# An adaLN block with dilated window attention and a token-mixing MLP: filling matmuls moved ahead of the first transposes, loads reordered, and a new issue order

## The chip, the cores and the metric

The kernel runs on one core of one Trainium2 chip. The metric is device microseconds of one execution, taken as the median of several runs. "Span" is the time from the first to the last instruction of one profiled execution; the time of a run is a little longer than its span.

The engines are named as the profile names them: PE multiplies matrices (PEld is its weight load), DVE, ACT and POOL work on elements, SP issues most of the DMA transfers. Each engine runs its own instructions in order and waits for the others through semaphores.

## The reference, cut to what matters

The input x has 2048 tokens of 512 features (bf16). A vector c gives six rows of modulation (scale, shift and gate for two branches).

```python
mod = (silu(c) @ w_mod).reshape(1, 6, 1, 512)
sa, ca, ga, sb, cb, gb = six rows of mod
h = layernorm(x) * (1 + ca) + sa
q, k, v = split(h @ wqkv)                  # 32 heads of 16
for each token: logits over 8 keys, at distances 0, 2, ..., 14 back
attn = softmax(logits * 16 ** -0.5)        # keys before the start are masked
x = x + ga * ((attn over v) @ wo)
h = layernorm(x) * (1 + cb) + sb
g = layernorm(h)
u = gelu(einsum('sd,sf->df', g, w1) + b1)  # mixes the 2048 tokens to 1792
y = einsum('df,fs->ds', u, w2) + b2        # and back to 2048 tokens
out = x + gb * y.T
```

## The kernel before, in words

Tokens are cut into 16 tiles of 128 and these into five chunks of 2, 4, 4, 4 and 2 tiles (`SIZES`, line 253). `build_chunk` (line 607) writes the work of one chunk:

- First layer norm: statistics (`ln1s`, on DVE, or with `:a` on ACT), reciprocal root on ACT (`rstd1_`, `rste1_`), then the normalised tile (`n1_`, on ACT, DVE or POOL).
- Transposition. Chunks 0 and 1 do it on PE (`tr0_0`, `tr1_0`, `tr1_2`), and the copy out of PSUM multiplies by `a1col`, the modulation scale plus one (`hT0_`, `hT1_`). Chunks 2 to 4 do it by transposing DMAs (`xt`), and use QKV weights that were multiplied by `a1col` instead (`wsc`).
- Projection on PE (`qkv{chunk}_{0 q, 1 k, 2 v}{part}`), copied out by ACT (`ev`). The q and v copies add a bias from the modulation shift (`qvb`, from `sab`).
- Scores: DVE multiplies q by eight shifted views of k (`qk`, four per chunk), and PE sums over a head (`red`). Softmax: max on DVE (`max`), subtracted on PE (`sub`), exponential on ACT (`exp`), sum on PE (`esum`), reciprocal on ACT (`rcp`, `rcq`), multiplied on DVE (`smB`).
- The softmax weights go through four DMAs to another layout (`a2_`), v through four others (`vd`). DVE multiplies them (`pv`, four per chunk), PE sums (`pvacc`), ACT copies (`oev`).
- Output projection with the residual (`wo`, `x1_`), second norm (`ln2`, `n2_`), modulation by rows (`aff`, `afb` on DVE), third norm (`ln3s`, `h3_`).

The MLP's first layer (`mlp1_{part}_{column block}_{first tile}`) needs tiles of `h3` as its reduction dimension, so its matmuls fill PE while the chunks run. Partial sums are parked in SBUF (`park`) and added later (`padd`); then `gelu`, then the second layer (`mlp2_`), the last arithmetic on DVE (`fin`) and the stores (`st_out`).

What sets the order is the string `ORDER` (line 180). Every step above is added to a graph by name, and `schedule` (line 87) checks that each name stands behind the names it depends on, picks PSUM and buffer slots in that order, and emits each step on its engine. A suffix picks an alternative: `:a`, `:d`, `:p` the engine, `:s` skip the step, `:q` write each product of 128 weight columns as four matmuls of 32 columns at four positions (`mm`, line 517). So each engine's queue, SP's DMA queue among them, is the list of names that fall to it, in the order of the string.

At the start, `ld_c` and the first x tiles are loaded, `cps` (one small matmul that turns c) leads to silu on ACT and DVE, and `modcols1`, `modcols0` (lines 553 and 556) multiply silu(c) with the modulation weights `ld_wmod1`, `ld_wmod0` for `a1col` and `sab`. The `warm` steps (line 523) are filling matmuls: they multiply the identity by itself, and nobody reads the product. `WARM` (line 267) gives how many matmuls each has. `warm0` is built apart (line 538): it stands behind `cps`, and by the key `wmA1` in front of `modcols1` and `modcols0`.

Of the kernel before, what the change touches and what calls it, by code (L numbers as in the profile page):

```python
# [180 lines left out]
halo0 ident ld_c act_table cps silu_exp ld_x1 ld_x0 ln1s0 ln1v0 ln1s1:a ln1v1 rstd1_0 rste1_0 ld_x_2_8 ld_x_1_2 nb1_0  # L181
consts ln1s9 silu_dve n1_1 n1_0:p tr0_0 ln1s8 ld_x_1_4 ln1s4:a ld_x_2_6 ln1s3:a warm0 ln1s5 ln1s7 ld_wmod1 ln1v5
ld_wmod0 modcols1 modcols0 ln1v9 ln1v8 ln1v4 ln1s2 ln1v2 ld_wqkv0 ln1v7 ln1v3 ln1s6 ln1v6 rstd1_1 rste1_1 nb1_1 n1_4:d
rstd1_2 rste1_2 n1_2:d n1_5:d nb1_2 ld_wqkv1 n1_3 n1_7 n1_6:d a1col hT0_2:d n1_9 tr1_2 tr1_0 hT1_1 wsc0_1:p hT0_1:d
sab hT0_0:d ld_x_3_12 hT0_3:d hT1_3:d qvb0 qvb_cp0 qkv0_00 warm6:s wsc1_3:a hT1_2:d qkv0_02 ev0_00 ld_wqkv2 qkv0_10
qkv0_12 ld_b2 ev0_10 ld_x_4_14 wsc1_2:p qkv0_20 wsc0_0 qvb1 ld_x_3_10 wsc0_3:p hT1_0:d ev0_02 wsc2_2:a ln1s13 ln1s12
ev0_12 ln1v12 ln1v13 wsc1_1:a qkv0_22 qk0_1 qkv1_13 ld_wmod2 ld_wo3 qk0_0 qk0_2 n1_8 red0_0 red0_1 ln1s11:a qkv1_03:q
qvb_cp1 qk0_3 xt6 red0_2 ld_wmod3 ev1_13 ev1_03 red0_3 mask wsc2_3:a ln1v11 ln1s10 ld_b1 ld_wo0 xt8 ev0_20 xt7 qkv1_11
ev1_11 ln1v10 max0 qkv1_01 ev1_01 rstd1_3 ev0_22 qk1_3 xt9 sub0 exp0 qkv1_00 ev1_00 qkv1_10 ev1_10 wsc1_0:a vd0_0
qk1_1 qkv1_02 esum0 rcp0 wsc0_2:p qk1_0 ev1_02 qkv1_12 qkv1_23 ld_wmod4 ld_wmod5 rcq0 ev1_12 qkv1_21 rste1_3 smB0  # L190
nb1_3 a2_0_0 ln1s15:a a2_0_2 qkv2_00 qk1_2 qkv2_10 n1_13:p red1_0 ev2_00 red1_1 ev2_10 red1_2 red1_3 ln1v15 a2_0_1
ev1_23 qkv2_13:q qk2_0 ev1_21 max1 modrow qkv1_20:q sub1:q ln1s14:a a2_0_3 pv0_0 wsc2_1:a halo_v1:a qkv1_22:q mrows
# [24 lines left out]
park0_8 ln2q13 pv4_3 park0_9 pvacc4_3 ld_w2_3 pv4_1 ld_w1_0_1664 oev4_2 pvacc4_0 ln2w12 warm4:s aff10 afb10 ld_w1_1_0
mlp1_0_12_6:q pvacc4_1 rstd2_12 rste2_12 nb2_12 n2_12:p ln3s10 mlp1_0_11_2:q oev4_0 ln3v10 wo15:q n2_13:p ld_row3
wo14:q mlp1_0_13_0:q mlp1_0_13_2:q ld_w2_0 x1_15:d ln3s11:a ln2m15 ln2q15 x1_14:d ln3v11 ln2w15 ln2m14 mlp1_0_11_6
mlp1_1_4_6 mlp1_0_13_6 aff12 ln2q14 rstd2_15 ln2w14 mlp1_1_1_6 afb12 rstd2_14 rste2_15 nb2_15 n2_15:p rste2_14  # L220
ld_w1_1_640 nb2_14 park0_10 warm5:s ln3s13 n2_14 ln3s12 rstd3_10 park0_11 aff14 rste3_10 ln3v13 park0_12 ln3v12
mlp1_1_2_6 afb14 aff15 rstd3_12 rste3_12 ln3s14 nb3_10 ln3v14 park0_13 mlp1_1_3_6 h3_10 rstd3_14 mlp1_1_0_6 afb15
ln3s15 ln3v15 mlp1_1_1_10 rstd3_15 rste3_15 mlp1_1_4_10 nb3_12:s rste3_14 mlp1_1_3_10 h3_13:d mlp1_1_0_10 mlp1_1_2_10
nb3_14:s h3_12:d mlp1_1_6_6 mlp1_1_6_10 nb3_15 h3_14:d padd1_0 mlp1_1_5_6 mlp1_1_5_10 h3_15 padd1_1 padd1_2 padd1_3
ld_w1_1_896 h3_11:p mlp1_1_7_10 padd1_7 gelu7 padd1_4 padd1_5 mlp1_1_8_10 mlp1_1_10_10 padd1_10 ld_w1_1_1408 padd1_6
ld_w1_2_0 big_done padd1_8 gelu10 mlp1_1_9_10 mlp1_1_11_10 mlp1_2_0_11 mlp1_2_2_11 mlp1_2_2_14 padd2_2 gelu8 padd1_9
# [12 lines left out]
def kernel(  # L239
# [24 lines left out]
    GRP=(2, 4, 4, 2, 1),  # L264
    XDMA=(2, 3, 4),
    INJ=(),
    WARM=(12, 2, 2, 2, 2, 2, 2, 2),
):
    nc = _OrderedNC(tc, 1)
    G = _Graph(dict(ps=6, big=NBIG, vd=NVD))  # L270
# [76 lines left out]
    add = G.add  # L347
# [681 lines left out]
```

## Time and profile before

| | |
|---|---|
| time, median of 3 runs | 198.08 us (197.78 to 198.33) |
| span of the profiled execution | 196.8 us |
| PE busy | 185.2 us (94%) |
| DVE busy | 156.6 us (80%) |
| ACT busy | 124.9 us (63%) |
| POOL busy | 19.9 us (10%) |
| chain of waits, by engine | PE 73%, DVE 13%, ACT 5%, issue 3%, DMA 2% |
| granted TensorE clock | 0.999 |

The profiled execution's own time is known only as its span; it is 1.3 us below the median of the runs. The busy time of PE counts the overlapped, modelled ends of matmuls, so 94% does not mean that PE works at its peak. In the page, a row of 40 digits cuts the span in slices of 4.92 us, and a digit is the busy share in tenths. In the timeline, the first column is the start and the second the length, from the start of the span; instructions that follow each other in one form are merged, "x12" is how many, and in brackets stands how long the engine was idle before and what released it. In the chain of waits, a row is start, length and what held the end at that time. Since almost every instruction is issued by one helper line (131), the tile names tell what an instruction is: `psS<-ident` a filling matmul, `big<-q_sb,k_f` a q·k product, `big<-a2sb,vD` a product with V, `lsb<-lsb,rb` the softmax multiply, `psS<-woq,o_sb` the output projection, `psS<-h,wst` and `psS<-gT,...` the MLP's two layers.

### The profile page before, as it was taken

To read this page: it belongs to the slowest core of one execution; us is meant where nothing else is said; L and a number is where in the kernel's file an instruction comes from. 1 tells how busy PE (TensorE), PEld (TensorE's weight loads), DVE (VectorE), ACT (ScalarE), POOL (GpSimd) and SP (SyncE) were. 2 spreads that over 40 slices of the span, in tenths; PEclk is the share of its full clock that TensorE was granted. 3 is DMA by queue.
4 is the path that set the end of the run, shared out by engine and by line. 5 is a ranking of instruction groups with operands and counts; after the bars stand their busy time and mean duration, and the time that the engine had idled before them with its cause. 6 is when DMAs were issued, how large, how long until landed. Compare 5 with 4: busy or idle time off the path is not lost.

```text
span 196.8 us, 4628 instructions
## 1 busy us (share of the span) xinstructions
PE 185.2 (94%) x1850; PEld 95.5 (48%) x1867; DVE 156.6 (80%) x244; ACT 124.9 (63%) x293; POOL 19.9 (10%) x38
## 2 busy tenths in 40 slices
PE   0699999999999999899999999999999999999994
PEld 0369554654444467244544454444444444444453
DVE  2888999999999999999999999965841633453664
ACT  6877999998999999999797889812760000000000
POOL 5123006320000005030000031200000000000000
PEclk9999999999999999999999999999999999999999
DMA  5998478778899732969674768888939293001112
GB/s 169 312 366 248 115 165 256 235 216 238 165 193 317 252 131 80 312 167 249 199 200 136 159 176 180 197 250 170 336 65 309 82 257 102 30 27 53 53 53 82
DMA packets 55369, 35.95 MB, mean 183 GB/s; under 512 B 24628, under 2 KB 52788, under 8 KB 55348
## 3 DMA queue, kind: packets, MB, share of 16 engines
q1 hardware_dynamic: 53468, 34.05, 63.2%
q10 hardware_dynamic: 1880, 1.61, 2.5%
q8 instruction: 14, 0.23, 0.5%
q14 instruction: 7, 0.06, 0.1%
HBM read 22.03 MB, written 2.10 MB: 123 GB/s over the span
## 4 chain that ended last, share of the span: by engine, by line
PE 73%; DVE 13%; ACT 5%; issue 3%; DMA 2%; SPq 1%; POOL 0%; DVEq 0%; ACTq 0%
PE psS L131 71%; DVE big L131 9%; DVE h L131 2%; PE psL L131 2%; ACT junk L131 1%; SPq L131 1%; DMA vD<-v_sb 1%; ACT xx L131 1%; DMA xx<-in_A_x_dram 1%; DVE m L131 1%; ACT o_sb L131 1%; ACT lsb L131 0%; DVE mv L131 0%; POOL h L131 0%; ACT v_sb L131 0%
## 5 line engine op out<-in xcount | busy, mean ns | idle before, releaser
L131 PEld LDWEIGHTS <-wst 128*128 128x128 bf16 (+1 forms) x566 | 35.5, 100 | 31.9 <-issue 1.3
L131 PE MATMUL psS<-h,wst 128*32 128x512 bf16 (+1 forms) x400 | 50.5, 379 | 0.4 <-issue 0.3
L131 DVE TENSOR_TENSOR big<-q_sb,k_f 128x4096 bf16<-128x4096 bf16 (+1 forms) x20 | 36.4, 1857 | 0.5 <-ACT k_f L131 0.5
L131 DVE TENSOR_TENSOR big<-a2sb,vD 128x4096 bf16<-128x4096 bf16 (+1 forms) x20 | 36.6, 1858 | 0.0
L131 DVE SCALAR_TENSOR_TENSOR h<-psS,bcol,rows_bc 128x512 f32<-128x512 f32 (+2 forms) x18 | 12.4, 690 | 24.2 <-PE psS L131 24.0
L131 PE MATMUL psS<-hT,w_qkv 128*32 128x512 bf16 (+3 forms) x414 | 28.7, 337 | 0.8 <-ACT v_sb L131 0.4
L131 PEld LDWEIGHTS <-w_qkv 128*32 128x32 bf16 (+1 forms) x462 | 19.9, 108 | 16.4 <-issue 2.7
L131 PE MATMUL psS<-gT,big 128*128 128x512 bf16 x109 | 24.3, 379 | 0.2
L131 POOL TENSOR_SCALAR h<-xx,rs,nb 128x512 bf16<-128x512 bf16 x6 | 10.6, 1777 | 84.2 <-DVE nb L131 84.2
L131 PEld LDWEIGHTS <-big 128*128 128x128 bf16 x144 | 12.0, 98 | 13.7 <-issue 0.5
L131 ACT ACTIVATE junk<-xx 128x512 bf16<-128x512 bf16 x28 | 17.7, 631 | 1.3 <-DVE xx L131 0.3
L131 ACT ACTIVATE h<-xx,nb,rs 128x512 bf16<-128x512 bf16 x22 | 17.2, 818 | 0.4 <-DVE nb L131 0.4
L131 PE MATMUL psS<-woq,o_sb 128*32 128x512 bf16 (+1 forms) x123 | 15.8, 380 | 0.4 <-ACT o_sb L131 0.4
L131 ACT ACTIVATE gT<-psS,bcol 128x512 bf16<-128x512 f32 x14 | 8.8, 686 | 10.6 <-DVE psS L131 10.6
L131 DVE TENSOR_TENSOR psS<-psS,gT 128x512 f32<-128x512 f32 x14 | 9.2, 695 | 6.3 <-PE psS L131 6.3
L131 DVE TENSOR_TENSOR h<-h,xx 128x512 bf16<-128x512 f32 (+2 forms) x18 | 11.4, 633 | 0.7
L131 ACT ACTIVATE q_sb<-psS,qvb 128x512 bf16<-128x512 f32 (+1 forms) x20 | 11.6, 603 | 0.3 <-PE psS L131 0.2
L131 PEld LDWEIGHTS <-group 128*32 128x32 bf16 x288 | 7.0, 96 | 9.8 <-issue 4.0
L131 PE MATMUL psS<-hT,wst 128*128 128x256 bf16 (+2 forms) x74 | 11.3, 333 | 0.1
L131 ACT ACTIVATE v_sb<-psS,qvb 128x512 bf16<-128x512 f32 (+1 forms) x20 | 11.2, 607 | 0.0
L131 DVE TENSOR_TENSOR h<-h,rows_bc 128x1024 bf16<-128x1024 bf16 (+2 forms) x14 | 10.5, 759 | 0.0
L131 ACT ACTIVATE k_f<-psS 128x512 bf16<-128x512 f32 x16 | 9.7, 606 | 1.1 <-PE psS L131 1.1
(90 smaller groups left out, 223.3 us busy)
## 6 DMA issues: line engine op xcount, KB each, us to landing
vD<-v_sb SPq DMA_DIRECT2D x12, 524.5 KB, 4.8
big<-in_B_w_dram SPq DMA_DIRECT2D x4, 896.0 KB, 7.5
vD<-v_sb SPq DMA_DIRECT2D x8, 268.5 KB, 3.1
wst<-in_B_w_dram SPq DMA_DIRECT2D x3, 640.0 KB, 5.4
xx<-in_A_x_dram SPq DMA_DIRECT2D x7, 256.0 KB, 5.6
wst<-in_B_w_dram SPq DMA_DIRECT2D x2, 800.0 KB, 4.7
gT<-in_w_mod_dram SPq DMA_DIRECT2D x3, 512.0 KB, 5.4
wst<-in_B_w_dram SPq DMA_DIRECT2D x2, 768.0 KB, 5.6
```

What stands on the lines that cost most here:

```text
L131: r = fn(*a, **k)
```

## The change

`WARM` goes from `(12, 2, ...)` to `(9, 1, 2, ...)`, `warm0` becomes a step like the others, without the key that held it in front of the modulation columns, and `ORDER` is replaced as a whole.

```diff
-    WARM=(12, 2, 2, 2, 2, 2, 2, 2),
+    WARM=(9, 1, 2, 2, 2, 2, 2, 2),
...
-        if w_ == 0:
-            f_warm0, s_w0 = f_warm, s_w
-            continue
...
-    add("pe", 0.216 * WARM[0], f_warm0, after=[G.ops[-1]], alloc=s_w0, frees=s_w0, writes=["wmA1"], name="warm0")
...
-    add("pe", 0.42, lambda: f_cols(1), reads=["sc", ("wmodA", 1), "wmA1"], writes=["wmA1"], alloc=s_m[1], name="modcols1")
+    add("pe", 0.42, lambda: f_cols(1), reads=["sc", ("wmodA", 1)], alloc=s_m[1], name="modcols1")
...
-    add("pe", 0.42, lambda: f_cols(0), reads=["sc", ("wmodA", 0), "wmA1"], frees=s_wm, alloc=s_m[0], name="modcols0")
+    add("pe", 0.42, lambda: f_cols(0), reads=["sc", ("wmodA", 0)], frees=s_wm, alloc=s_m[0], name="modcols0")
```

The start of the two strings, cut to the first lines (all of the rest differs too):

```diff
-halo0 ident ld_c act_table cps silu_exp ld_x1 ld_x0 ln1s0 ln1v0 ln1s1:a ln1v1 rstd1_0 rste1_0 ld_x_2_8 ld_x_1_2 nb1_0
-consts ln1s9 silu_dve n1_1 n1_0:p tr0_0 ln1s8 ld_x_1_4 ln1s4:a ld_x_2_6 ln1s3:a warm0 ln1s5 ln1s7 ld_wmod1 ln1v5
-ld_wmod0 modcols1 modcols0 ln1v9 ln1v8 ln1v4 ln1s2 ln1v2 ld_wqkv0 ln1v7 ln1v3 ln1s6 ln1v6 rstd1_1 rste1_1 nb1_1 n1_4:d
...
+ident ld_c cps act_table silu_exp ld_x0 ld_x1 ln1s0:a silu_dve ln1s1 ln1v1 ln1v0 ld_x_1_4 rstd1_0 rste1_0 ln1s4 nb1_0
+ln1s5 ld_x_1_2 ln1s2 ln1s3 ln1v2 ld_wmod1 ln1v5 consts n1_1 ln1v3 ln1v4 rstd1_1 rste1_1 ld_x_2_8 n1_0:p ld_x_2_6
+ld_wqkv1 warm0 tr0_0 nb1_1 n1_2 ln1s8:a ld_wmod0 ld_wqkv0 warm1 modcols1 a1col ld_x_3_10 ld_x_3_12 n1_5:d n1_3:d hT0_0
+n1_4:p ld_b1 wsc1_0:p warm2 tr1_2 ld_wqkv2 hT0_3:d ln1s6 hT0_2:d hT0_1:d ln1s7 ln1v8 wsc1_2:p tr1_0 ln1v7 ld_x_4_14
+qkv0_10 hT1_2 ln1s9 hT1_0 ln1v6 ln1v9 qkv0_12 modcols0 hT1_3 rstd1_2 rste1_2 ld_b2 hT1_1:d nb1_2 ev0_10 n1_9:d qkv1_10
...
```

What the new order does, in the words of the steps:

- Loads on SP: x0, x1, x tiles 4 and 5, 2 and 3, `wmod1`, x tiles 8 and 9, 6 and 7, `wqkv1` (K), `wmod0`, `wqkv0` (Q). Before: x1, x0, 8 and 9, 2 and 3, 4 and 5, 6 and 7, `wmod1`, `wmod0`, `wqkv0`, `wqkv1`.
- PE: `cps`, `warm0` (9 matmuls), `tr0_0`, `warm1` (1), `modcols1`, `warm2` (2), `tr1_2`, `tr1_0`, then the K projection of chunk 0 ahead of `modcols0` and of Q. Before: `cps`, `tr0_0`, `warm0` (12), `modcols1`, `modcols0`, `tr1_2`, `tr1_0`, `qvb0`, Q, K. The skipped `warm` steps stand at the end of the string, and the two matmuls of `warm1` behind the last product are gone.
- More steps are written with `:q`: 1829 matmuls of 32 columns and 561 of 128, for 1129 and 738. Neighbours on PE whose width differs go from 26 to 4.
- Engines: the norms `n1_4`, `n1_7`, `n1_8`, `n1_11`, `n2_0`, `n2_2`, `h3_13` and `h3_15` move to POOL, `n1_13` and `n2_5` leave it; `halo0` moves behind `n1_8` on POOL. Some statistics, norms, column scalings (`hT`) and weight scalings trade between DVE and ACT; `ev0_12` moves to DVE.
- `qk1_0` stands ahead of `max0` on DVE, `woq_s` ahead of the first `pv`. `mlp2` tiles, `st_out` stores and the late W1 and W2 loads stand in another order; the last tile's three pieces keep theirs.

101 lines of the change are left out of this document (50 added, 51 removed).

## The prediction

> **What bounds the kernel now.** I read the page first (the busy shares and the 40 slices), then the windows by stage, the chain of waits, and at last the timeline at each place where the chain changes engine.
>
> ```profile
> span 196.8 us, 4628 instructions
> DVE  2888999999999999999999999965841633453664
> ```
> ```profile
> 2.00:8.00 6.00, 1.71 (x11) 1.23 (x12) 3.65 (x10) 4.92 (x13) 2.06 (x14) 1.00 0.92 277
> 8.00:13.00 5.00, 5.00 (x38) 2.14 (x37) 4.29 (x19) 4.12 (x13) 0.00 (x0) 1.00 1.08 371
> 18.00:42.00 24.00, 23.63 (x305) 13.82 (x310) 23.89 (x23) 23.45 (x53) 5.90 (x2) 1.00 0.65 174
> 42.00:82.80 40.80, 39.12 (x605) 20.57 (x604) 40.73 (x34) 39.24 (x93) 2.90 (x2) 1.00 0.80 217
> 82.80:193.80 111.00, 110.33 (x833) 52.70 (x842) 78.88 (x145) 49.18 (x121) 5.11 (x6) 1.00 0.59 157
> ```
> ```profile
> 6.47 10.88 PE psS L131 x108
> ...
> 18.07 1.79 DVE big L131 x2
> ...
> 36.91 1.22 DVE big L131
> ...
> 82.77 7.30 PE psS L131 x33
> ```
> ```profile
> 184.51 9.30 PE L131 MATMUL psS<-gT,wst 128*128 128x512 bf16 x70
> ```
>
> A window's row gives PE, PEld, DVE, ACT and POOL busy, then clock, DMA share and GB/s. There are three regimes. Until 18 the loads feed everything (DMA share 0.92 and 1.08). From 18 to 82.8 DVE never rests (23.89 of 24.00, 40.73 of 40.80). From 82.8 to the last matmul (184.51 + 9.30 = 193.8) PE is busy 110.33 of 111.00, and 3.0 us of output work follow. DVE's slices (4.92 us each) stay full until about 125 us, so the two are in balance: PE's gain counts only as far as DVE's chain comes earlier too.
>
> **The change part by part.** Every sum is made against the profiled span of 196.8; the median of the runs, 198.08, stands 1.3 above it, and I carry the difference over unchanged.
>
> *The filling matmuls.*
>
> ```profile
> 2.20 0.18 PE L131 MATMUL psS<-ident,c_t 4*128 4x4 bf16 x1 [2.20 <-DMA c_t<-in_c_dram]
> ...
> 5.64 0.77 POOL L131 TENSOR_SCALAR h<-xx,rs,nb 128x512 bf16<-128x512 bf16 x1 [2.11 <-DVE nb L131]
> ...
> 6.47 1.03 PE L131 MATMUL psS<-ident,h 128*128 128x128 bf16 x8 [4.09 <-POOL h L131]
> ...
> 7.30 5.20 PE L131 MATMUL psS<-ident 128*128 128x512 bf16 x12
> ...
> 12.33 0.94 PE L131 MATMUL psS<-sc,big 128*128 128x1 bf16 x32
> ...
> 13.13 1.05 PE L131 MATMUL psS<-ident,h 128*128 128x128 bf16 x16
> ...
> 14.02 0.67 PE L131 MATMUL psS<-sab,wst 128*128 128x1 bf16 x16
> ...
> 14.55 3.66 PE L131 MATMUL psS<-hT,wst 128*128 128x256 bf16 x32
> ...
> 18.07 3.50 DVE L131 TENSOR_TENSOR big<-q_sb,k_f 128x2048 bf16<-128x2048 bf16 x3 [0.51 <-ACT k_f L131]
> ```
>
> Before, twelve fillers of 0.43 us (5.20/12) stand between the first transposes and the modulation columns. After, nine stand behind the silu product: 2.4 + 9 x 0.43 = 6.3, inside PE's wait of 4.09 for the first normalised tile at 6.42. They cost nothing; were that tile 0.2 us earlier, they would begin to. Three more fillers stand in gaps where PE waits for loads. So 5.2 us leave PE's path, and what is late next is the loads.
>
> *The loads.*
>
> ```profile
> wst<-in_A_wqkv_dram SPq DMA_DIRECT2D x2, 512.0 KB, 8.3
> ```
>
> They land in issue order at 277 GB/s to 8 and 371 after. Before, the first QKV weight is complete at 2.88 MB: by these rates 11.3, by its landing (issued at 4.8, 8.3 median less 0.5) 12.6, so completion lags 1.3. After, the modulation weights for the scale complete at 1.31 MB (8.0), the K weights at 2.36 MB (11.2), the Q weights at 3.41 MB (14.0). K of chunk 0 so starts at 11.2, 3.3 ahead of the first projection now (14.55); but Q must wait for its bias product at 14.5, and runs 15.0 to 16.0. Its copy on ACT (behind one K copy, one norm and one weight scaling) ends at 17.3. DVE's own queue ahead of the first q·k product, counted in the instruction orders, holds 11 statistics instead of 9 and one K copy more, three norms and four column scalings instead of four and seven: 0.2 us more in all. Starting 0.6 earlier and waiting as long, it is there at 17.7. **First q·k: 17.7 for 18.07, -0.4**, though PE then has nearly three projections of chunk 1 behind it (0.87 each at 217 ns for 512 columns, below) that it has not begun now: some 2 us ahead.
>
> *First softmax and first products with V.*
>
> ```profile
> L131 DVE TENSOR_TENSOR big<-q_sb,k_f 128x4096 bf16<-128x4096 bf16 x12 | 27.1, 2284 | 0.0
> ```
> ```profile
> 30.82 0.42 DVE L131 TENSOR_TENSOR lsb<-lsb,rb 128x512 bf16<-128x512 bf16 x1
> ```
> ```profile
> 31.27 2.70 SPq L131 DMA_DIRECT2D a2sb<-lsb  x4
> ```
> ```profile
> a2sb<-lsb SPq DMA_DIRECT2D x12, 64.0 KB, 3.3
> ...
> a2sb<-lsb SPq DMA_DIRECT2D x8, 32.0 KB, 2.5
> ```
>
> The new order puts one 2.28 us product ahead of the first max, but takes it from behind it: by the sum of the rows of its queue DVE reaches the softmax multiply at 30.2 for 30.82. Then the weights go out by SP, 0.67 us an issue (2.70/4), now with one V transfer between: the fifth issue starts at 30.65 + 4 x 0.67 = 33.3 and lands 2.5 later, 35.8. DVE has one product, the scaling of wo and a max meanwhile (4.6 us, to 35.2) and waits 0.6. **First product with V: 35.9 for 36.91, -1.0.**
>
> *To the first place where PE stays full.*
>
> ```profile
> 78.88 2.29 DVE L131 TENSOR_TENSOR big<-a2sb,vD 128x4096 bf16<-128x4096 bf16 x1
> ...
> 82.77 0.82 PE L131 MATMUL psS<-woq,o_sb 128*128 128x512 bf16 x3 [0.37 <-ACT o_sb L131]
> ```
> ```profile
> 57.15 0.59 PE L131 MATMUL psL<-m,nident 128*128 128x512 bf16 x2
> 57.68 1.05 PE L131 MATMUL psS<-big,group 128*32 128x512 bf16 x16
> 58.55 0.39 PE L131 MATMUL psS<-hT,w_qkv 128*32 128x512 bf16 x4
> ```
>
> Between the first product with V and chunk 2's last, both orders give DVE 44.3 us of work: each instruction at its row's mean less the 0.07 by which it overlaps the next (a q·k or V product of 4096 columns at 2.21). The new order has one q·k more there (2.2), and the scaling of wo and one max less (1.1 each), which stand earlier or later. So that product ends 1.0 earlier (81.2 now, 78.88 + 2.29), and so does the wo that waits for its copy. Sixteen narrow matmuls, four products of 512 columns, take 0.87 (57.68 to 58.55), 0.217 each; two full ones before a change of width take 0.53, so a change costs 0.10. The narrow form (:q) itself costs nothing. Behind the first wo of this chunk stand 110.9 us of matmuls in both orders. Changes of width fall from 26 to 4 in the instruction order; of those left in the row of 111 us, four go: 0.4. **End by this place: -1.0 - 0.4 = -1.4.**
>
> *Chunks 3 and 4.*
>
> ```profile
> 101.89 0.62 PE L131 MATMUL psS<-big,group 128*32 128x512 bf16 x8
> ```
> ```profile
> 97.35 4.49 DVE L131 TENSOR_TENSOR big<-a2sb,vD 128x4096 bf16<-128x4096 bf16 x2
> ...
> 111.35 3.49 DVE L131 TENSOR_TENSOR big<-a2sb,vD 128x2048 bf16<-128x2048 bf16 x3
> ```
> ```profile
> 115.08 0.39 PE L131 MATMUL psS<-big,group 128*32 128x256 bf16 x8
> ```
>
> Chunk 3's products with V now follow its softmax after 4.3 us of DVE work; the four transfers need 3 x 0.67 plus 2.5 to 3.3, 4.5 to 5.3. I take 0.5 of waiting, from 0.2 to 1.0. From the first product with V to chunk 3's last DVE has 65.9 us for 65.4, since a max (1.1) now falls behind chunk 2's last product and a norm and small work (0.6) ahead of it or to ACT. So it arrives where it did (-1.0 + 0.5 + 0.5), at 101.84, and PE takes it up at 101.89, without slack. Behind it stand 91.0 us of matmuls for 91.8 (four first-layer products more are done by then), and three changes of width go: -1.1. For chunk 4 DVE arrives 0.1 earlier, had 0.24 of slack (114.84 against 115.08), and PE has 78.4 for 78.9 and one change less: -0.95. The latest of the three sets the end: **-0.95, call it -1.0.**
>
> *At nothing.*
>
> ```profile
> 125.69 0.41 DVE L131 TENSOR_SCALAR h<-h,mv,rs 128x512 bf16<-128x512 bf16 x1
> ```
> ```profile
> wst<-in_B_w_dram SPq DMA_DIRECT2D x3, 320.0 KB, 5.3
> ```
>
> The last norm ends near 126.1 with 65.5 us of matmuls behind it, 191.6 of 193.8: a slack of 2.2 covers the three last norms now on POOL (about 1 us). The last W1 load, of 320 KB, becomes free to go 23 matmuls, 5.0 us, ahead of its use and lands in 5.3; matmuls that run slightly late cover the rest, and without them it costs 0.3. The other W1 and W2 loads stand further ahead. The stores change queues, but the last three pieces keep their order: the 3.0 us tail stays. ACT gives up five norms and takes three column scalings; it is not late at any of these places.
>
> *The norms moved to POOL* (six more in balance).
>
> ```profile
> 31.42 4.91 POOL L131 TENSOR_SCALAR h<-xx,rs,nb 128x512 bf16<-128x512 bf16 x1 [15.17 <-DVE nb L131]
> ```
>
> Alone such a norm took 0.77, beside DVE's products 4.91. The ones that DVE or the transposes wait for soon stand beside a reduction or statistics, so I take 0.8 to 1.0; at 4.91 each could hold DVE up to 4 us once. The Trainium skill ("GPSIMD Engine Reference", Specifications) says that POOL shares its SBUF interfaces with VectorE and contends with instructions of two SBUF inputs; the trace agrees at 4.91 against 0.77, and by that rule alone each of the six would cost 4 us of POOL time, most of it off the path.
>
> **The rivals.**
>
> *PE counts in full (larger gain).* The head start of 2 us, 22 changes of width (2.2) and nothing lost to DVE give 198.1 - 4.2 = 193.9. DVE's 40.73 of 40.80 speaks against it; half of it, 196, would need a DVE that waits less at 9 to 17 than I have it.
>
> *Handed back (no change).* The a2 wait of chunk 3 at 1.0 and a DVE that reaches the first q·k at 18.0: 198.0.
>
> *SP in the way (slower).*
>
> ```profile
> 20.41 1.32 SPq L131 DMA_TRANSPOSE hT<-h  x1
> ```
>
> In chunks 1 and 2 a transposing transfer stands among the four a2 transfers (6.7 us of DVE work to cover them). It takes 1.32 us of SP's queue. If SP is held for longer, DVE waits at the first product with V of each chunk: three waits of 1.0 give +3.0 - 1.0, 200.1. Two waits of 0.5 are the point from which it decides.
>
> *The clock comes late (slower).* The first fillers and transposes run at 0.43 us for 512 columns, and a transpose takes 0.129 at 6.47 (1.03/8) but 0.066 at 13.13 (1.05/16). So PE, at work without a pause from 6.47, is fast only some 6 us later. After, it starts at 2.4 and pauses near 6.3, 7.8 and 9. If it is still slow at 11.2 and for 6 us on, the 4.4 us of projections up to the first Q take some 2.4 more (the wait for the Q weights hides the rest), and so does everything behind: 199.5. It decides when the clock opens after 11.2. The Trainium skill ("TensorE: Matmul & The Clock Gate", Part 1) states that a free-running window of some 3.4 us must be busy before the clock opens, wherever it lies. By that rule the pauses could cost one window, and this rival would come; no row here shows a window with pauses.
>
> **How the numbers follow.** Forecast 0.42, PE in full or in part 0.18, handed back 0.12, SP 0.17, clock 0.11. A run tells 0.3%, 0.6 us, from no change. A fifth of the forecast's chance lies above 197.5, within 0.3%: faster 0.34 + 0.18 = 0.52, same 0.08 + 0.12 = 0.20, slower 0.28. The likeliest is 198.08 - 1.0 = 197.1. The forecast's own bounds (0.2 to 1.0 at chunk 3, 0.7 at the first q·k either way) give 196.0 to 198.0. Reaching for half of the first rival and most of the slow ones: 194.8 to 199.8.
>
> **What would show it.** Right: PE's fillers end near 6.3, K projection at 11 to 11.5, first q·k near 17.7, first product with V near 36, chunk 2's first wo near 81.8, PE full from there. Wrong: projections at 0.43 us per 512 columns after 11; DVE idle before V products by more than 1; chunk 2's first wo before 80 or after 83.

## The result, and the profile after

The changed kernel takes **207.04 us** (median of 4 runs, 205.85 to 209.05) where the kernel before takes 198.21 (4 runs, 197.78 to 198.73): a ratio of 1.042, 95% interval 1.038 to 1.046. The forecast was 197.1, within 194.8 to 199.8, so the sign was wrong and the range did not hold it. Below, ratios are to the kernel before on the same chip; executions more than 1.5% above the fastest of their kernel stay in the medians but are left out of the ratios (for e15 its runs are given).

The page of the kernel after, with its span, its slices for DVE and for the granted clock, its chain by engine, and its row for the products with V:

```profile
span 205.4 us, 5687 instructions
DVE  3579998899949999998699999987571244465664
PEclk9969999999997899969999999999999999999999
PE 55%; DVE 12%; DMA 12%; ACT 9%; SPq 5%; issue 5%; DVEq 0%; ACTq 0%
L131 DVE TENSOR_TENSOR big<-a2sb,vD 128x4096 bf16<-128x4096 bf16 (+1 forms) x20 | 36.7, 1861 | 5.6 <-DMA vD<-v_sb 2.9
```

The third row shows the clock below full in three places. DMA now carries 12% of the chain, and DVE stood idle 5.6 us ahead of the products with V, for none of which it waits in the trace of before. The windows by stage (PE, PEld, DVE, ACT, POOL busy, then clock, DMA share, GB/s):

```profile
2.00:8.00 6.00, 4.91 (x19) 1.84 (x19) 4.38 (x15) 3.90 (x10) 1.91 (x14) 1.00 0.85 250
8.00:13.00 5.00, 3.43 (x35) 2.40 (x36) 1.82 (x6) 3.65 (x10) 1.25 (x2) 0.70 1.08 377
42.00:88.50 46.50, 39.59 (x816) 24.43 (x816) 42.94 (x33) 38.53 (x93) 5.65 (x2) 0.96 0.75 211
88.50:202.40 113.90, 112.83 (x1059) 54.48 (x1062) 80.34 (x148) 48.89 (x116) 7.41 (x9) 0.99 0.53 144
```

In the middle stage DVE works 42.94 of 46.50, for 40.73 of 40.80. The chain of waits names what it waited for:

```profile
3.22 7.04 DMA xx<-in_A_x_dram
...
24.45 5.41 DMA gT<-in_w_mod_dram
...
36.54 3.23 DMA vD<-v_sb
...
51.57 8.56 DMA vD<-v_sb
60.18 0.04 issue
60.22 2.29 DVE big L131
...
88.08 0.63 PE psL L131 x8
88.70 8.17 PE psS L131 x144
```

Before, the chain held two transfers, x at the start for 2.16 and a V transfer at 34.01 for 2.48. Now it holds four, for 24.2 us. The timeline of DVE at the same places as in the prediction, and of PE behind the long wait:

```profile
19.14 2.47 DVE L131 TENSOR_TENSOR big<-q_sb,k_f 128x2048 bf16<-128x2048 bf16 x2
...
31.66 0.42 DVE L131 TENSOR_TENSOR lsb<-lsb,rb 128x512 bf16<-128x512 bf16 x1
...
35.41 1.22 DVE L131 TENSOR_TENSOR woq<-woq,rows_bc 128x2048 bf16<-128x2048 bf16 x1 [0.88 <-DMA rows_bc<-mrows]
...
38.77 4.63 DVE L131 TENSOR_TENSOR big<-a2sb,vD 128x2048 bf16<-128x2048 bf16 x4 [0.93 <-DMA a2sb<-lsb]
...
60.22 2.29 DVE L131 TENSOR_TENSOR big<-a2sb,vD 128x4096 bf16<-128x4096 bf16 x1 [2.86 <-DMA vD<-v_sb]
...
64.23 2.28 DVE L131 TENSOR_TENSOR big<-a2sb,vD 128x4096 bf16<-128x4096 bf16 x1
```
```profile
63.77 0.62 PE L131 MATMUL psL<-m,nident 128*32 128x512 bf16 x8 [2.86 <-DVE m L131]
...
88.51 1.90 PE L131 MATMUL psS<-woq,o_sb 128*32 128x512 bf16 x16
```

In before, chunk 1's last product with V is this row:

```profile
58.71 2.28 DVE L131 TENSOR_TENSOR big<-a2sb,vD 128x4096 bf16<-128x4096 bf16 x1
```

From these rows and those of before comes the bill for the two profiled executions (the span is 8.6 longer):

| place | before | after | later by |
|---|---|---|---|
| first q·k product | 18.07 | 19.14 | 1.07 |
| softmax multiply of chunk 0 | 30.82 | 31.66 | 0.84 |
| first product with V | 36.91 | 38.77 | 1.86 |
| end of chunk 1's last product with V | 60.99 | 66.51 | 5.52 |
| chunk 2's first wo | 82.77 | 88.51 | 5.74 |
| end of the span | 196.8 | 205.4 | 8.6 |

So there are four places: 1.1 at the start, 1.0 between the softmax and the first product with V, 3.7 in chunk 1 (the wait of 2.86, and 1.0 for the q·k product that stands here now and the scaling of wo that doesn't), 2.9 behind chunk 2's first wo. At three of them lies a fall of the clock. The windows cut at the clock's own steps:

```profile
6.63:10.04 3.41, 1.30 (x26) 0.94 (x26) 1.21 (x7) 1.32 (x3) 0.77 (x1) 1.00 1.00 341
10.04:13.46 3.42, 2.88 (x20) 1.89 (x18) 2.11 (x7) 3.08 (x8) 0.94 (x2) 0.50 1.09 383
61.25:64.66 3.41, 0.89 (x20) 0.51 (x23) 3.41 (x5) 2.04 (x4) 0.77 (x1) 1.00 1.02 298
64.66:68.07 3.41, 3.41 (x40) 1.59 (x36) 3.31 (x3) 2.71 (x5) 0.00 (x0) 0.50 0.98 301
85.14:88.55 3.41, 1.30 (x24) 0.38 (x24) 3.41 (x3) 3.41 (x9) 2.39 (x1) 1.00 1.14 301
88.55:91.96 3.41, 3.41 (x40) 1.36 (x40) 3.38 (x6) 2.63 (x6) 2.56 (x3) 0.50 0.43 171
```

Three times a stretch of 3.41 us in which PE worked 0.9 to 1.3 is followed by one of 3.41 us at half clock. The last one stands on PE's full row: half of 3.41, 1.7, is lost there.

### The profile page after: what moved, and what is told of

Read it like the earlier page. It is cut to its first block, busy times and chain, and to the rows that moved or that the text cites. A ratio compares the mean times of both kernels' runs of the same rounds, so it can differ in the third digit from the quotient of the medians.

```text
span 205.4 us, 5687 instructions
## 1 busy us (share of the span) xinstructions
PE 188.7 (92%) x2381; PEld 101.5 (49%) x2390; DVE 156.9 (76%) x243; ACT 122.5 (60%) x285; POOL 24.0 (12%) x45
## 4 chain that ended last, share of the span: by engine, by line
PE 55%; DVE 12%; DMA 12%; ACT 9%; SPq 5%; issue 5%; DVEq 0%; ACTq 0%
PE psS L131 54%; DVE big L131 8%; DMA vD<-v_sb 6%; SPq L131 5%; ACT junk L131 4%; DMA xx<-in_A_x_dram 3%; DMA gT<-in_w_mod_dram 3%; DVE h L131 2%; DVE m L131 1%; ACT q_sb L131 1%; ACT xx L131 1%; ACT k_f L131 1%; PE psL L131 1%; ACT o_sb L131 1%; DVE hT L131 0%
## 5 line engine op out<-in xcount | busy, mean ns | idle before, releaser
L131 PEld LDWEIGHTS <-wst 128*32 128x32 bf16 (+1 forms) x692 | 36.2, 100 | 32.0 <-issue 1.2
L131 PE MATMUL psS<-hT,w_qkv 128*32 128x512 bf16 (+1 forms) x576 | 30.4, 357 | 0.0
L131 PEld LDWEIGHTS <-w_qkv 128*32 128x32 bf16 (+1 forms) x618 | 22.6, 108 | 13.7 <-issue 1.4
L131 POOL TENSOR_SCALAR h<-xx,rs,nb 128x512 bf16<-128x512 bf16 x10 | 12.1, 1208 | 88.9 <-DVE nb L131 69.7
L131 PE MATMUL psS<-woq,o_sb 128*32 128x512 bf16 (+1 forms) x232 | 17.8, 410 | 0.0
L131 ACT ACTIVATE junk<-xx 128x512 bf16<-128x512 bf16 x26 | 16.4, 630 | 1.6 <-DMA xx<-in_A_x_dram 1.1
L131 ACT ACTIVATE h<-xx,nb,rs 128x512 bf16<-128x512 bf16 x17 | 13.7, 820 | 4.0 <-DVE nb L131 4.0
L131 PE MATMUL psS<-big,group 128*32 128x512 bf16 (+1 forms) x160 | 10.3, 339 | 4.2 <-DVE big L131 4.2
L131 PE MATMUL psS<-hT,wst 128*32 128x512 bf16 (+2 forms) x98 | 11.7, 347 | 0.8 <-DVE hT L131 0.7
L131 PEld LDWEIGHTS <-o_sb 128*32 128x32 bf16 (+1 forms) x232 | 7.4, 103 | 7.4 <-issue 1.5
## 6 DMA issues: line engine op xcount, KB each, us to landing
vD<-v_sb SPq DMA_DIRECT2D x12, 524.5 KB, 5.8
```

The lines of the kernel that those rows point to most:

```text
L131: r = fn(*a, **k)
```

## The experiments

My theory after reading: the time went (a) into transfers that stand in line behind others on SP and in the DMA queue (W1 ahead of V in chunk 1, a row and loads ahead of the softmax weights in chunk 0), (b) into the clock, which falls where PE pauses, (c) at the start, into ACT waiting for tiles of x. The rivals: the bandwidth is short whatever the order; the half clock is hidden or has another cause; or the narrow matmuls have a price of their own.

**e1: W1 behind V.**

```diff
-ld_w1_0_0 pvacc1_0 ev3_02 ev3_01 vd1_1 red2_2 red2_3 vd1_3
+pvacc1_0 ev3_02 ev3_01 vd1_1 red2_2 red2_3 vd1_3 ld_w1_0_0
```

> Kernel after, one SP transfer moved: the 768 KB load of W1 that stands ahead of chunk 1's last two V transfers goes behind them. Theory (queue order on SP and in the DMA rings): V of chunk 1 lands some 4 us after its issue, as the others do, instead of 8.56; DVE's wait of 2.86 at 60.22 falls below 0.5, PE's wait of 2.86 behind it goes too, and the time falls by 2 to 3, from 207.0 to 204.0-205.0. Rival (the bandwidth is short at 50 to 60 whatever the order): V lands where it did, within 0.7 us, DVE still waits 2 or more, and the time stays at 206.5-207.5.

Measured: 202.36 (201.57 to 204.29), ratio 1.021 [1.015, 1.027], for 1.042. One transfer moved by two places gives back 4.7 of the 8.8. SP's timeline, first of after, then of e1:

```profile
50.92 0.61 SPq L131 DMA_DIRECT2D wst<-in_B_w_dram  x1
51.57 1.23 SPq L131 DMA_DIRECT2D vD<-v_sb  x2
```
```profile
50.57 1.26 SPq L131 DMA_DIRECT2D vD<-v_sb  x2
51.87 0.86 SPq L131 DMA_DIRECT2D wst<-in_B_w_dram  x1
```

In e1 the first of these V transfers lands 3.2 us after its issue, not 8.56, and DVE and PE do not wait. The third product of chunk 1 with V:

```profile
56.79 2.28 DVE L131 TENSOR_TENSOR big<-a2sb,vD 128x4096 bf16<-128x4096 bf16 x1
```

This execution has no half clock at all (its mean is 1.000). At the times of the two last falls of after:

```profile
64.66:68.07 3.41, 3.41 (x70) 1.75 (x64) 3.41 (x3) 3.35 (x10) 0.00 (x0) 1.00 0.83 191
88.55:91.96 3.41, 3.41 (x72) 1.73 (x64) 3.41 (x10) 3.35 (x11) 0.00 (x0) 1.00 0.14 52
```

The rival of short bandwidth falls: the same bytes go at the same time. The gain is larger than expected (2 to 3). Of the 4.9 between the two profiled spans, 0.5 stand ahead of the first product with V, which the edit doesn't touch; 2.9 are the wait; 0.2 more come up to chunk 2's first wo, and 1.3 behind it, where after lost 1.7 to the clock. This last part can't be put down to the transfer: e8, e9 and e11 (below), built on e1 and without a wait for V in chunk 1, fall there again. The windows of e8:

```profile
80.75:84.16 3.41, 1.23 (x16) 0.34 (x17) 3.41 (x3) 3.41 (x9) 3.24 (x1) 1.00 1.11 268
84.16:87.57 3.41, 3.04 (x32) 1.31 (x35) 3.38 (x6) 2.27 (x5) 1.72 (x2) 0.50 0.63 245
```

So the moved transfer is worth some 3 by the traces. The rest of the 4.7 comes with executions in which the clock stays up: two of e1's four runs have a clock of 0.999 or more, and no run of after is above 0.973.

**e2: PE's pauses filled.** Eleven fillers among chunk 2's last reductions, in the kernel after.

```diff
-ev4_12 pvacc2_3
+ev4_12 warm3 pvacc2_3
...
-ld_w2_1 pvacc2_0 sub3:q
+ld_w2_1 warm4 pvacc2_0 warm5 sub3:q
...
-    WARM=(9, 1, 2, 2, 2, 2, 2, 2),
+    WARM=(9, 1, 2, 3, 6, 2, 2, 2),
```

> Kernel after, with filling matmuls of 0.22 us put into PE's waits for chunk 2's last products with V: three ahead of the third reduction, six ahead of the fourth, two ahead of the masking for chunk 3's softmax (gaps of 0.89, 1.59 and 0.52 in the trace of after). Theory (the granted clock falls to half because PE stood idle, and stays there for 3.41 us): no half rate from 88.5 to 92, and the time falls by 1.5 to 2.0, from 207.0 to 205.0-205.5. Rival (the half rate has another cause, or its work was hidden): half rate as before or no gain, 206.5-207.5.

Measured: 207.87 (204.53 to 208.57), ratio 1.038 [1.029, 1.047]: no gain in the time. The clock did stay up at this place, in the window that begins with chunk 2's first wo:

```profile
91.70:203.70 112.00, 111.13 (x1059) 54.10 (x1058) 79.72 (x147) 48.48 (x116) 7.41 (x9) 1.00 0.52 141
```

The same 1059 matmuls took 1.7 less than after's 112.83, which is the half of 3.41. But this execution, at 208.57 the slowest of the four, had come there 3.2 later (91.69): it had two half windows at the start, 9.58 to 16.41, and waited longer in chunks 0 and 2. The mean clock of the four runs is 0.983 to 0.991, for 0.964 to 0.973 in after, and the median is no lower. So the clock's price behind chunk 2 is shown in the trace; that filling alone makes the kernel faster is not.

**e3, e6: the fillers by themselves, in the kernel before.** e3 takes only this part of the change; e6 adds fillers until PE has hardly a pause.

```diff
-n1_1 n1_0:p tr0_0 ln1s8
+n1_1 n1_0:p warm0 tr0_0 ln1s8
...
-ln1s3:a warm0 ln1s5
+ln1s3:a ln1s5
...
-ld_wmod0 modcols1 modcols0
+ld_wmod0 warm1 modcols1 modcols0
...
-n1_9 tr1_2
+n1_9 warm2 tr1_2
...
-    WARM=(12, 2, 2, 2, 2, 2, 2, 2),
+    WARM=(9, 1, 2, 2, 2, 2, 2, 2),
```

> Kernel before, with the part of the change that concerns the fillers alone: nine ahead of the first transposes and one and two in the next gaps, instead of twelve behind the transposes; loads and every other order as before. The prediction's theory: 5.2 us leave PE's path, loads are late next, first q.k product at 17.0 to 17.7 for 18.07, time 197.2-197.8 for 198.2. Rival (the clock): the pauses at 7 to 10 let the granted clock fall to half for 3.4 us near 10, the projections of chunk 0 run late, first q.k at 18.0 or later, time 198.0-198.8.

> Kernel before with the fillers ahead of the transposes as in e3, and four more behind the first transposes and two between the two groups of modulation columns, so that PE has hardly a pause from 2.3 on. Theory (e3 lost its 1.5 us because the clock fell back in the pauses; and the twelve fillers of before cost nothing, since the weights land at 12.6 and 14.1 anyway): the clock does not fall between 8 and 15, the first q.k product is at 17.8-18.2 as in before, time within 0.4 of it, 198.0-198.7. The prediction's step 1 (5.2 us leave PE's path and count until the loads are late): first q.k 17.0-17.7, time 197.2-197.9. Rival (the fillers' place costs by itself): 199.5 or more, as e3.

e3 measured 199.87 (10 runs, 199.07 to 201.12), ratio 1.009 [1.006, 1.011]: **this part alone makes the kernel slower,** by more than its rival expected. One half window takes 1.7 of 197, 0.009, off the mean clock: two of the ten runs have 0.991, one half window, and eight 0.980 to 0.983, two. Its windows at the clock's steps, and its first q·k product:

```profile
8.18:11.59 3.41, 0.73 (x23) 0.64 (x24) 3.34 (x15) 2.51 (x9) 0.00 (x0) 1.00 1.06 358
11.59:15.01 3.42, 3.42 (x51) 2.87 (x48) 2.34 (x10) 2.26 (x4) 1.28 (x2) 0.50 1.10 356
```
```profile
18.47 2.36 DVE L131 TENSOR_TENSOR big<-q_sb,k_f 128x2048 bf16<-128x2048 bf16 x2 [0.68 <-ACT k_f L131]
```

e6 (`warm1` at 5, and `warm3` ahead of `modcols0`) measured 199.08 (12 runs, 197.91 to 200.33), ratio 1.003 [1.000, 1.006]. Its runs fall into two groups by the granted clock: the five at 1.00 took 197.91 to 198.25 (median 198.01), the seven at 0.99 took 198.99 to 200.33 (median 199.40). One half window at the start costs 1.4 us, and where there is none, the kernel stands where before does (198.16 in the same runs). So taking the fillers off PE's path gave nothing to speak of; the Q and K weights of before land at 12.6 and 14.1 in any case (issued at 4.8 and 5.3, 7.8 and 8.8 to landing). e6's profiled execution fell although PE had worked 2.19 of 3.41:

```profile
9.22:12.63 3.41, 2.19 (x43) 1.47 (x44) 3.31 (x15) 2.68 (x9) 0.00 (x0) 1.00 1.08 372
12.63:16.05 3.42, 3.42 (x38) 2.90 (x36) 2.84 (x10) 2.07 (x4) 2.27 (x4) 0.50 1.10 349
```

**e4: the tiles of x ahead of the modulation weights, in the kernel after.**

```diff
-ld_wmod1 ln1v5 consts n1_1 ln1v3 ln1v4 rstd1_1 rste1_1 ld_x_2_8 n1_0:p ld_x_2_6
+ld_x_2_8 ld_x_2_6 ld_wmod1 ln1v5 consts n1_1 ln1v3 ln1v4 rstd1_1 rste1_1 n1_0:p
```

> Kernel after, with the two loads of x that ACT and POOL wait for near 10 us put back ahead of the modulation weights. Theory (ACT, held by these statistics until 11.66, makes the first q.k late): ACT's first copy to hT by 11.2, first q.k at 18.4-18.7 for 19.14, time 206.3-206.7. Rival (the modulation weights, some 1.3 us later now, hold the scaled copies as long; or the half clock at 10.0 to 13.5 does): first q.k at 19.0-19.6, time 206.8-207.5.

Measured: 205.97 (203.59 to 207.80), ratio 1.028 [1.024, 1.033]; first q·k at 18.67, inside the expectation, the time lower than expected. But that the moved loads gave the 0.5 is not shown: e1, whose list at the start is that of after, has its first q·k at 18.23; there the same loads landed 0.9 earlier (below) and the clock stayed up. And the rest of the gain isn't the start's: in this execution V landed at 58.04 instead of 60.13 and DVE waited 0.38 instead of 2.86, although the list is the same there. So single traces differ at places where a transfer is just late.

**e7: the narrow form by itself, in the kernel before.** 579 more matmuls, the order untouched; one of the steps:

```diff
-qk3_0 wo3 ev3_03
+qk3_0 wo3:q ev3_03
```

> Kernel before, with every matmul that after issues as four narrow ones of 32 columns issued so too; no order changed. Changes of matmul width fall from 26 to 8 (18 at 0.10), matmuls rise from 1867 to 2446. The prediction (a change costs 0.10, the narrow form nothing, and only changes on PE's full stretch count): four to six of them, 0.3 to 0.6 faster, 197.8-198.1 for 198.4. Rival 'PE counts in full': 1.5 to 1.8 faster, 196.6-196.9. Rival 'the narrow form has a price of its own (four weight loads for one)': slower by 0.5 or more, 198.9 and up.

Measured: 198.75 (12 runs), ratio 1.002 [1.000, 1.004]: no gain from 18 changes of width fewer. The stretch from chunk 2's first wo in this kernel:

```profile
82.41:194.36 111.95, 111.70 (x1099) 54.20 (x1086) 79.81 (x150) 49.61 (x122) 5.11 (x6) 1.00 0.58 158
```

In before:

```profile
82.77:194.20 111.43, 110.77 (x834) 52.73 (x842) 79.31 (x146) 49.21 (x121) 5.11 (x6) 1.00 0.59 158
```

The wo of e7 comes 0.36 earlier, but the row behind it is 0.5 longer. By these two traces the narrow form has a price about as large as what it saves in changes of width; neither was measured alone.

**e5, e9, e12: chunk 0's handover.** In e1 the first product with V still comes at 38.29, 7.6 us behind the multiply (before: 6.1). Three kernels on the base of e1 rearrange it; in all three the scaling of wo moves as shown for e5.

```diff
 e5
-ev1_12 exp0 rstd1_3
+ev1_12 exp0 ev0_22 rstd1_3
...
-ld_wo3 modrow xt9
+ld_wo3 modrow vd0_2 vd0_3 xt9
...
-xt7 smB0 nb1_3
+xt7 smB0 a2_0_2 a2_0_1 a2_0_0 a2_0_3 vd0_0 vd0_1 ld_row0 nb1_3
...
-qkv1_22:q ld_row0 ev0_22 a2_0_2 biascols_cp woq_s qkv1_21:q a2_0_1
+qkv1_22:q biascols_cp qkv1_21:q
...
-qk2_3 xt11
+qk2_3 woq_s xt11
 e9
-xt7 smB0 nb1_3
+xt7 smB0 a2_0_2 a2_0_1 a2_0_0 a2_0_3 nb1_3
...
-n1_11:p vd0_2 qkv1_23:q a2_0_0 a2_0_3
+n1_11:p vd0_2 ld_row0 qkv1_23:q
 e12, e5 but for this
-modrow vd0_2 vd0_3 xt9
+modrow xt9
...
-xt7 smB0
+xt7 vd0_2 vd0_3 smB0
```

> Kernel e1 (W1 behind chunk 1's V) with chunk 0's handover to its products with V put back as before: the copy of V earlier on ACT, two V transfers ahead of the softmax weights and two behind, the weights' four transfers one behind the other and ahead of the row for wo, and the scaling of wo behind the products. Theory (the first product with V is late, 38.29 for 36.91, because a row, a V transfer and two waits of DVE stand ahead of it): first product with V at 35.9-36.4, less 1.2 for the scaling that comes later, end 0.8 to 1.3 earlier than e1's 202.4: 201.1-201.6. Rival (ACT, with one copy of V more ahead of the softmax, hands it over later): first product with V at 37.5 or later, time 202.4-203.5.

> Kernel e1 (W1 behind chunk 1's V), with the four transfers of chunk 0's softmax weights one behind the other as soon as the weights are there; the first V transfer, the row for wo, the other V transfers and the scaling of wo (behind the next q.k product) follow. Nothing else moves (in e5 two V transfers ahead of SP's transposing ones held everything). Theory (first product with V late because a row and a V transfer stand among the weights): weights landed by 35.7-36.2 for 38.1, first product with V at 36.3-37.2 for 38.29; the scaling of wo (1.2) now comes behind it, so the end gains 0.3-0.8: 201.6-202.1 for e1's 202.4. Rival (the copy of V on ACT is what is late): first product with V at 38 or later, time 203 or more.

> Kernel e1 (W1 behind chunk 1's V), with chunk 0's handover as in e5, but with the two early V transfers behind SP's three transposing ones instead of ahead of them: V's copy on ACT follows the exp, then on SP three transposing transfers, two of V, the four of the softmax weights, the other two of V, the row; the scaling of wo behind the next q.k product. Theory (e9 and e11 showed that the weights are in time, landed by 36 with the softmax at 30.4, and that V behind them is not, at 37.8): first product with V 5.3-6.0 behind the softmax multiply instead of 7.6, so at 35.9-36.7; less 1.2 for the scaling that comes later, the end gains 0.5-1.0 on e1's 202.4: 201.4-201.9. Rival (ACT, which now has V's copy of 0.84 ahead of the softmax, hands the weights over later by as much, or the gain is lost in the next waits): multiply at 31.3 or later, or first product with V as early as said and the time 202.2 or more.

All three missed: 207.18 (ratio 1.041 [1.035, 1.047]), 204.13 (1.027 [1.022, 1.031]) and 204.11 (1.028 [1.025, 1.032]). The timelines of DVE, of e5 and then of e9:

```profile
42.31 3.50 DVE L131 TENSOR_TENSOR big<-a2sb,vD 128x2048 bf16<-128x2048 bf16 x3 [3.22 <-DMA a2sb<-lsb]
```
```profile
39.86 4.63 DVE L131 TENSOR_TENSOR big<-a2sb,vD 128x2048 bf16<-128x2048 bf16 x4 [1.97 <-DMA vD<-v_sb]
```

In e5 the two V transfers waited on SP until 30.80 and held the three transposing ones, 1.3 to 2.1 each, behind which the weights went out at 38.04 only. In e9 the weights were in time and V behind them was not (landed 39.77, multiply at 32.41). In e12 the two V transfers took 1.56 and 1.77 to issue, the weights went out at 33.93, and the first product came at 39.16, 7.4 behind the multiply.

**e13, e14, e15: SP's whole list there as in before.** On the base of e12: the three transposing transfers first, then the modulation weights, V, the softmax weights, V, two loads of wo; the matmuls of the modulation rows behind. e14 adds e4's loads and six fillers for one at the start; e15 moves the rows' matmuls and chunk 1's weights once more.

```diff
 e13
-mask xt6
+mask xt6 xt9 xt8 xt7
...
-ev1_03 ld_wo2 rcp0 ld_wo3 modrow xt9
+ev1_03 rcp0
...
-vd0_0 vd0_1 ld_row0 nb1_3
+vd0_0 vd0_1 ld_wo2 ld_wo3 nb1_3
...
-esum1:q pvacc0_0 pvacc0_1 ev2_00
+esum1:q modrow mrows ld_row0 pvacc0_0 pvacc0_1 ev2_00
 e15
-esum1:q modrow mrows ld_row0 pvacc0_0 pvacc0_1 ev2_00
+esum1:q pvacc0_0 pvacc0_1 ev2_00 modrow mrows ld_row0
...
-smB1 ev2_11
+smB1 a2_1_0 a2_1_3 a2_1_1 a2_1_2 ev2_11
```

> Kernel e1 (W1 behind chunk 1's V), with SP's whole list between 22 and 45 as in before: the three transposing transfers first, then two loads of the modulation weights, V, the softmax weights, V, two loads of wo, the modulation rows and their matmuls behind the sum of chunk 1's softmax, the scaling of wo behind the next q.k product. Theory (after loads 1.0 MB of modulation weights and 0.13 MB of wo ahead of the transposing transfers, which then land 7 to 8 us behind their issue and everything behind them late): transposing transfers landed by 28-29, first product with V 5.0-5.8 behind the softmax multiply instead of 7.6; with the scaling of wo (1.2) behind it the end gains 0.5-1.2 on e1: 201.2-201.9. Rival (what is gained there is lost in the next waits, as in e9, e10 and e12): 202.2 or more, with new DVE waits of 0.5 and up behind.

> Kernel e13 with the loads of x ahead of the modulation weights and six fillers for one behind the first transposes (the start's part of e8). Theory: first q.k at 17.9-18.1 as in e8, clock up from 8 in most executions, otherwise as e13: 0.2-0.6 faster than it, 200.8-201.5. Rival: no difference to e13 within 0.5.

> Kernel e14, in which PE met the matmuls of the modulation rows ahead of the reductions of chunk 0's products with V (DVE waited 2.35 for a free buffer at 42.33, PE 0.85 for the copy of the rows). Here these matmuls stand behind two of those reductions, and chunk 1's four transfers of softmax weights ahead of SP's transposing ones (DVE waited 1.46 for them at 54.43). Theory (the gain at the first product with V, 3 us against e1, reaches the end once these two new waits are gone): both waits below 0.5, chunk 1's last product ends at 61.5-62.5, time 200.5-201.5. Rival (another wait takes their place): chunk 1's last product ends at 63 or later, time 202.5 or more.

Measured: 206.42 (ratio 1.042 [1.035, 1.048]), 204.85 (1.032 [1.026, 1.038]) and 205.83 (runs of 203.71, 204.49, 207.16 and 207.44; 1.041 [1.034, 1.049], by the two faster runs 1.030). The place itself came out as the theory has it: in e13 5.2 behind the multiply, in e14 at 35.35, 5.0 behind it and 1.6 earlier than in before. But the gain does not arrive. DVE's timeline of e14, then of e15:

```profile
35.35 4.63 DVE L131 TENSOR_TENSOR big<-a2sb,vD 128x2048 bf16<-128x2048 bf16 x4 [0.29 <-DMA a2sb<-lsb]
...
42.33 2.29 DVE L131 TENSOR_TENSOR big<-q_sb,k_f 128x4096 bf16<-128x4096 bf16 x1 [2.35 <-ACT q_sb L131]
...
54.43 2.29 DVE L131 TENSOR_TENSOR big<-a2sb,vD 128x4096 bf16<-128x4096 bf16 x1 [1.46 <-DMA a2sb<-lsb]
```
```profile
44.42 0.69 DVE L131 TENSOR_TENSOR lsb<-lsb,rb 128x1024 bf16<-128x1024 bf16 x1 [2.11 <-ACT rb L131]
...
58.53 2.29 DVE L131 TENSOR_TENSOR big<-a2sb,vD 128x4096 bf16<-128x4096 bf16 x1 [1.14 <-PE psS L131]
```

Each wait taken away is followed by another of about its size: the rival of these three runs.

**e8, e10, e11: chunk 3, and several at once.** In e1 chunk 3's softmax multiply comes 5.1 behind chunk 2's first wo (before: 0.9), and DVE waits 1.25 at the first product with V. e10 starts that softmax one product earlier; e8 moves one first-layer product behind the last reduction and takes e4's loads and six fillers; e11 joins e9, e10 and that start.

```diff
 e10
-n2_3 pv2_0 max3
+n2_3 max3 pv2_0
...
-ld_w2_1 pvacc2_0 sub3:q
+ld_w2_1 sub3:q exp3 pvacc2_0
...
-wo7:q exp3 x1_7 wo8:q esum3:q wo9:q afb2
+esum3:q rcp3 rcq3 wo7:q x1_7 wo8:q wo9:q afb2 smB3
 e8
-mlp1_0_1_2:q qk4_3 red4_3
+qk4_3 red4_3 mlp1_0_1_2:q
```

> Kernel e1 (W1 behind chunk 1's V) with three repairs more: the two loads of x ahead of the modulation weights (as e4), six fillers instead of one behind the first transposes (the clock stays up), and one product of the first layer behind the last reduction of chunk 4's scores, which DVE waits for 1.25 at chunk 3's first product with V. Theory (the waits found in the traces add up along DVE): first q.k 17.9-18.2, chunk 3's first product with V waits 0.5 instead of 1.25, time 200.8-201.6 for e1's 202.4. Rival (what is gained ahead of the first product with V is lost in its waits for the transfers): 202.0-202.6.

> Kernel e1, with chunk 3's softmax started one product with V earlier (its max ahead of chunk 2's last product, the masking, exp and sum ahead of the projections of the output, the last multiply ahead of the statistics), as in before. Theory (the multiply comes at 90.06 in e1, 5.1 behind the first wo, for 0.9 in before; so the weights land after DVE is ready and DVE waits 1.25, and PE behind it 1.0): multiply at 86-87.5, wait at chunk 3's first product with V below 0.3, end 0.9-1.4 earlier, 201.0-201.5. Rival (a reduction that PE reaches late, behind 56 narrow matmuls, ends that wait): wait still 1.0 or more, 202.0-202.6.

> Kernel e1 with the edits of e9 and e10, the loads of x of e4, and six fillers for one behind the first transposes. Theory (the late points are separate and add up): first q.k 17.9-18.2, first product with V 36.3-37, no wait at chunk 3, time 200.0-200.8. Rival (PE's own row of matmuls behind chunk 2, 1 us longer than before's in the narrow form, and one DVE wait turned into the next, keep it): 201.5 or more.

Measured: 203.48 (1.025 [1.020, 1.029]), 204.15 (1.024 [1.018, 1.031]) and 203.99 (1.027 [1.023, 1.031]): none beats e1 (1.021). The comparison is blurred by the clock: the profiled execution of e1 has no half window, those of e8 and e11 have one at chunk 2's end. In e10 the wait at the product did go, and a new one of 1.09 stands at the multiply:

```profile
88.48 1.01 DVE L131 TENSOR_TENSOR lsb<-lsb,rb 128x1024 bf16<-128x1024 bf16 x1 [1.09 <-ACT rb L131]
```

The single executions with a clock of 0.998 or more are free of this: e1 201.57 and 202.16, e5 204.54, e8 201.54, e10 201.91 and 203.74, e11 202.90, e12 202.98, e14 204.35 and 204.48, e15 203.71. None is clear of e1 to the better, and no kernel built on the new order comes near before's 198.

## Why the prediction was wrong

The forecast's span is 195.8 (196.8 - 1.0), the profiled one 205.4. Of the 9.6 between them, 1.4 had come up by the first q·k, 1.4 more by the first product with V, 3.8 more by chunk 2's first wo, and 2.9 behind it.

**The fillers (5.2 us leave PE's path).** They ended at 6.6, hidden as forecast, and "what is late next is the loads" was right too; but then nothing was to be had. In before the loads are as late, and the twelve fillers stand in front of weights that land at 12.6 and 14.1; e6 without a fall of the clock equals before. What the step took for waste kept PE busy, and without it the clock fell in all ten runs of e3.

**The loads.** In the trace of after all of them came 1.1 to 1.5 later than the sum by rates: PE had the modulation weights at 9.49 for 8.0, POOL the K weights at 12.52 for 11.2, the Q weights landed at 15.13 for 14.0. The stretch from 2 to 8 ran at 250 GB/s for the 277 taken. The tiles of x that moved behind these weights weren't priced: ACT waited for them until 10.28, and the copies that scale the transposes stand behind them on ACT. First q·k 19.14 for 17.7. Most of this is no fault of the sum: in e1, with the same list, the weights came at 8.65, 11.62 and 14.2, ACT had its tile at 9.38, and the first q·k stands at 18.23, 0.5 behind the forecast and 0.2 behind before; its clock stayed up, too. What made the loads 0.9 later in after's execution is open.

**The clock rival** had 0.11. That pauses of PE cost the clock is right, but its condition was wrong: not that the clock opens after 11.2 (it opened at 6.63) but that it falls again, and in after that slowed the transposes (10.04 to 13.46) and of the projections only the first matmul, at 12.52. Its price by itself is what e6 measured, 1.4 for one half window at the start.

**First product with V (35.9; measured 38.77).** The step had the softmax at 30.2 and a fifth issue at 33.3. The softmax came at 31.66. Then SP sent the row for wo first, and the fifth issue started at 35.20. It landed 3.4 later, not 2.5, with a V transfer in front of it. The step counted the scaling of wo as cover for DVE and overlooked its row on SP. e13 and e14 show that SP's list makes this place late: with before's list the product comes 5.2 and 5.0 behind the multiply, for 7.1 in after.

**DVE's 44.3 in both orders, so PE's full row starts 1.0 earlier (81.8; measured 88.51).** This is the step that failed most. The work was counted rightly: in e1 it is 82.73 - 38.29 = 44.4, in after 86.89 - 38.77 = 48.1. What it left out is that DVE must have its data: W1 was priced "at nothing" by its own need date, not by what stands behind it in the same queue. That costs 2.86. The fall of the clock at chunk 2's end (1.7) comes on top; the step counted on a full clock there, and e8, e9 and e11 show the fall without W1 in the way. The rival "SP in the way" (0.17) foresaw DVE waits at the products with V, three of 1.0 by transposing transfers. There were three, 0.93, 2.86 and 1.66 (chunk 3), the longest by W1.

**Changes of width (-0.4).** Not seen: e7 has 18 fewer and is not faster. That the narrow form costs nothing, on which the step rests, was read from sixteen matmuls; e7's row, with 1099 matmuls for 834, is 0.5 longer.

**Chunk 3's wait (0.5, 0.2 to 1.0).** 1.66 in after, 1.25 in e1. e10 shows that even without it the next wait takes its place. DVE's work up to chunk 3's last product was taken as 65.4 and 65.9; it is busy 64.80 in before and 65.67 in e1, 0.9 more and not 0.5.

**PE's 110.9 behind chunk 2's first wo, in both orders.** Right to 0.4 once the clock is up: 111.13 busy in e2, 110.77 in before. So of the 2.9 lost behind this place 1.7 is the half clock and 0.4 this difference; the other 0.8 was not taken apart.

**Norms on POOL.** Right for the time: ten at 1.2 on average in after's page, none on the chain. One of the moved ones, at 82.65 beside DVE's products with V, took 4.89 and not 0.8 to 1.0.

**What stays open.** e1 is 4 us slower than before. By the two traces chunk 3's products with V end 3.9 later in it: 1.4 stand at the first product with V, 1.7 are waits of DVE from there on, and 0.9 is one q·k product more in this stretch, less the scaling of wo. The first and the last of these waits were removed without a gain. The waits can be named, but an order of ACT, PE and SP together that avoids them was not found, so the cause of these 4 us stays open.

## What to carry to other kernels

Price a load by what stands behind it in its queue and not only by the date at which it is used: one of 768 KB ahead of two of 524.5 KB that DVE needed next cost 2.9 us. Before you take filling matmuls away, ask what is late next: here it was the loads, and the fillers in front of them cost nothing and kept the clock up. When two kernels are compared by their traces, compare the clock first: a half window that falls in one execution and not in the other is 1.4 to 1.7 us that need not come from the edit. In an order written by hand in which four engines and a queue are in balance, a wait removed alone moves to the next engine; look for the whole list that stood at that place before.

## What the runs showed of the hardware

The clock works in stretches of 3.41 us that lie on a grid: the three falls of after, at 10.04, 64.66 and 88.55, are 16 and 7 such stretches apart. The grid does not begin with the kernel: with the same list at the start, the eight transposes from 6.51 took 0.66 in after, whose clock opened at 6.63, and those from 6.43 still 1.03 in e1. This first opening is read from durations alone, since the clock of the rows doesn't show it: before's twelve fillers take 0.43 each, for 0.217 later, in a window (8 to 13) whose clock reads 1.00. It falls not only when PE is idle for a whole stretch. The Trainium skill ("TensorE: Matmul & The Clock Gate", Part 1) has half rate after at least one idle window of about 3.4 us; here windows with 0.89 and 1.30 of 3.41 busy were enough, and at the start even one with 2.19 in e6 and one with 2.23 in e2, while in e1 two at the start with 2.15 and 2.07 did not fall. Later in the kernel windows like this one of e12 did not fall either:

```profile
82.50:85.91 3.41, 1.68 (x32) 0.54 (x24) 3.41 (x3) 3.41 (x9) 2.58 (x1) 1.00 1.09 308
```

So no single busy time, as the profile counts it, decides. The same kernel falls in one execution and not in the next, which in e6 is the larger part of the scatter (198.0 or 199.4). That the place of the grid decides it is likely, and no run tests it.
